# W_gate and W_up ahead of W_Q: another order of the first three loads and of their products in an attention and feed-forward decode kernel

## The chip, the cores and the metric

The kernel runs on one core of a Trainium2 chip. The metric is the device time of one execution in microseconds (us); the time before is a median of three runs.

## The reference

One token of each of 4 sequences goes through a layer norm, and the normed row `xn` feeds two branches that are added to the input:

```python
xn = _layernorm(x, axis=-1)                       # x: (4, 1, 512)
return x + _A_ref(xn, A_k_cache, A_v_cache, A_wq, A_wo) + _B_ref(xn, B_w_gate, B_w_up, B_w_down)
# A: q = xn @ wq; k, v = last W = 4096 rows of the caches, 8 heads, each shared by 4 query heads
#    softmax(q k^T / sqrt(128)) v, then @ wo        (32 query heads of 128)
# B: (silu(xn @ w_gate) * (xn @ w_up)) @ w_down     (F = 1792)
```

All tensors are bf16. The keys and values that are read are 8 heads x 4 sequences x 4096 rows x 128 numbers each, 32 MiB for the keys and as much for the values; the weights add some 14 MB.

## The kernel before, in words

The work goes in eight groups, one for each key/value head (`HKV = 8`, named 1 to 8 on the computing engines and 0 to 7 on the loading side, where K0 and V0 are the loads of the first group). A group's keys are 4 MiB in one of two buffers `kbuf`, its values 4 MiB in one of two buffers `vbuf`. The loads are all issued by SyncE (SP in the profile) in `on_sync`, in program order on one queue: W_Q (L256), W_gate (L257), W_up (L258), then `load(g)` for g = 0 to 7 (keys at L241, the last head's in two halves at L245 and L246, values at L251), then W_down (L261, L263) and W_O in five pieces (L254). Two buffers are used twice: W_Q lies in the second value buffer (`WQ` is a view of `VB1`), and W_O in the first key buffer.

SP waits in three places. Before the keys of head g >= 2 it waits until the transposes of head g - 2 are done (`s_tr`), before the values of head g >= 2 until that head's value products are done (`s_pv`), and before the values of head 1, which overwrite W_Q, until the query products are done (`s_q`, L248). The input row X is loaded by ScalarE (ACT) at L271.

VectorE (DVE) and ACT compute the layer norm (L306 to L312), TensorE (PE) transposes it (L377), DVE copies it to `XnT` (L314). Then come the three products with a weight that stands on its own semaphore each, in `on_tensor`: the queries (L381 to L386: wait for W_Q, 4 x 32 matmuls into `q_ps`, then `s_q`), and in one loop gate and up (L387 to L399: for each weight a wait and 21 x 4 matmuls into `gate_ps` and `up_ps`, then `s_gu`). A row of W_Q in a partition is 4 x 4096 bf16 numbers, 32 KB without a gap; one of W_gate or W_up is 4 x 1792 numbers, 14 KB.

DVE takes the queries out of PSUM in two copies after waiting for `s_q` (L315 to L319: `QT` for all heads and `QC` for the first group), then, after ACT's exponential of the gate (L290), forms the SwiGLU product `guT` in four steps (L355 to L362). PE waits for `guT` (L404) before its loop over the groups.

In a group PE transposes the keys in 16 chunks (L415) into PSUM, DVE and ACT share the copies of them to SBUF (L326 and L280), PE forms the scores (L427), a maximum is taken and subtracted, ACT takes the exponential (L283), and PE multiplies with the values (L448). Between the steps PE runs filler matmuls (`spin`, L470). After the groups come the down product (L474), a permutation of the heads (L528), the product with W_O (L474 and L478), two copies to `y`, and the store (L302).

## Time and profile before

| | |
|---|---|
| time, median of 3 runs | 195.13 us (195.11 to 195.15) |
| time of the profiled execution | 195.3 us |
| its span, first to last instruction | 193.9 us |
| bytes read from HBM | 81.01 MB, 418 GB/s over the span |
| busy share of the span | PE 84%, DVE 51%, ACT 36%, POOL 3% |
| mean granted clock of PE | 0.991 |

The page cuts the span into 40 slices of 4.85 us. Digits are busy shares in tenths. Beside them stands what the 16 DMA engines moved in each slice. The chain of work is followed backward from the last instruction and given in order of time: a start, a length, and what ran or was waited for. In a timeline a row is a start, a length, an engine, a line, an operation with the tile written and the tiles read, and in square brackets the idle time of the engine before it with what ended it. A row of a load names its queue (SPq) and the time that issuing took; its landing is found among the DMA issues, in us after the issue. Rows of a wait name who waited, for whom, the us in total, the times, and the longest. Rows of a stretch (windows) give the limits, the length, the busy time of the five engines, the granted clock, the DMA share and GB/s.

### The profile page before, as it was taken

The numbers are of one execution on the slowest core, as the hardware profiler recorded it, in microseconds if no ns is written. First come the engines' busy times: TensorE is split into PE (matmuls) and PEld (weight loads), VectorE is DVE, ScalarE is ACT, GpSimd is POOL, SyncE is SP. The second block draws the span as 40 slices with busy tenths as digits, with TensorE's granted clock in tenths as the row PEclk, the third lists the DMA queues.
The fourth block names the chain that finished last, engine by engine and source line by source line (L and its number), as shares of the span: only waits on it lengthen the run. The fifth ranks groups of instructions, "written<-read, shape, count | busy, mean of one in ns | idle before, by whom it ended". The sixth has DMA issues, their size and how long they took to land.

```text
span 193.9 us, 6951 instructions
## 1 busy us (share of the span) xinstructions
PE 163.8 (84%) x3179; PEld 135.2 (70%) x3179; DVE 99.0 (51%) x200; ACT 69.1 (36%) x100; POOL 5.7 (3%) x33
## 2 busy tenths in 40 slices
PE   0038973998699899999999799989996999999995
PEld 0038973997389759956994699469945994997532
DVE  0200011578258737870885188428842884588230
ACT  5510000243416343525461446234623462363421
POOL 7300000000000000000000000000000000000000
PEclk9999999999789999999999999999999999999999
DMA  6999999999999999999999999999999999999993
GB/s 216 433 438 429 427 429 433 429 433 429 433 429 436 426 429 436 426 433 433 439 433 433 433 433 433 433 433 433 433 433 433 433 426 433 439 433 433 436 400 131
DMA packets 3800, 81.14 MB, mean 418 GB/s; under 512 B 440, under 2 KB 576, under 8 KB 832
## 3 DMA queue, kind: packets, MB, share of 16 engines
q1 hardware_dynamic: 3776, 81.00, 97.5%
q8 instruction: 8, 0.13, 0.2%
q10 hardware_dynamic: 16, 0.01, 0.0%
HBM read 81.01 MB, written 0.00 MB: 418 GB/s over the span
## 4 chain that ended last, share of the span: by engine, by line
PE 48%; DMA 44%; DVE 5%; issue 1%; SPq 1%; ACT 0%; DVEq 0%
DMA kbuf<-in_A_k_cache_dram 44%; PE ps_kt L415 23%; PE ps_s L427 8%; PE ps_o L448 5%; PE ps_kt L470 4%; DVE kT L326 2%; PE ps_s L439 2%; PE ps_s L464 2%; DVE mx L332 2%; PE ps_s L478 1%; PE ps_s L474 1%; PE ps_s L461 1%; PE ps_kt L454 1%; PE ps_kt L434 0%; ACT s L298 0%
## 5 line engine op out<-in xcount | busy, mean ns | idle before, releaser
L415 PE MATMUL ps_kt<-ident,kbuf 128*128 128x128 bf16 x1024 | 78.2, 224 | 9.0 <-DMA kbuf<-in_A_k_cache_dram 8.5
L415 PEld LDWEIGHTS ps_kt<-ident,kbuf 128*128 128x128 bf16 x1024 | 60.6, 100 | 11.2 <-DMA kbuf<-in_A_k_cache_dram 9.6
L326 DVE COPY kT<-ps_kt 128x1024 bf16<-128x1024 bf16 x88 | 57.6, 686 | 18.5 <-PE ps_kt L415 16.5
L280 ACT ACTIVATE kT<-ps_kt 128x1024 bf16<-128x1024 bf16 x40 | 40.9, 1023 | 52.9 <-PE ps_kt L415 52.9
L427 PE MATMUL ps_s<-qC,kT 128*128 128x16 bf16 x1024 | 44.8, 170 | 2.6 <-DVE kT L326 1.9
L427 PEld LDWEIGHTS ps_s<-qC,kT 128*128 128x128 bf16 x1024 | 38.4, 97 | 4.6 <-DVE kT L326 4.1
L283 ACT ACTIVATE p<-ps_s 128x512 bf16<-128x512 f32 x32 | 16.5, 603 | 34.0 <-PE ps_s L439 34.0
L332 DVE TENSOR_REDUCE mx<-ps_s 128x16 f32<-128x512 f32 x32 | 22.0, 689 | 6.9 <-PE ps_s L427 5.0
L470 PE MATMUL ps_kt<-own,ones 128*128 128x512 bf16 x82 | 20.7, 380 | 0.0
L448 PE MATMUL ps_o<-vbuf,p 128*32 128x256 bf16 x512 | 19.1, 289 | 0.3
L448 PEld LDWEIGHTS ps_o<-vbuf,p 128*32 128x32 bf16 x512 | 14.9, 101 | 5.9 <-ACT p L283 4.2
L343 DVE TENSOR_REDUCE dsum<-ps_kt 128x16 f32<-128x256 f32 x8 | 3.4, 425 | 28.6 <-PE ps_kt L454 28.6
L454 PE MATMUL ps_kt<-p,ones 128*32 128x256 bf16 x64 | 16.9, 287 | 0.0
L470 PEld LDWEIGHTS ps_kt<-own,ones 128*128 128x128 bf16 x82 | 6.6, 97 | 7.0 <-issue 1.1
L377 PE MATMUL ps_s<-i,xn 4*128 4x4 f32 x4 | 0.6, 254 | 10.1 <-DVE xn L312 10.1
L439 PE MATMUL ps_s<-cm,own 128*128 128x512 bf16 x32 | 8.3, 380 | 1.0 <-DVE cm L340 1.0
L377 PEld LDWEIGHTS ps_s<-i,xn 4*128 4x128 f32 x4 | 0.6, 208 | 10.1 <-issue 10.1
L454 PEld LDWEIGHTS ps_kt<-p,ones 128*32 128x32 bf16 x64 | 6.6, 103 | 0.1
L290 ACT ACTIVATE ex<-ps_o 128x84 f32<-128x84 f32 x1 | 0.2, 240 | 17.5 <-PE ps_o L396 17.5
L439 PEld LDWEIGHTS ps_s<-cm,own 128*128 128x128 bf16 x32 | 2.5, 97 | 5.3 <-DVE cm L340 3.4
L286 ACT ACTIVATE osb<-ps_o 128x256 f32<-128x256 f32 x8 | 3.1, 383 | 8.2 <-PE ps_kt L454 8.2
L464 PE MATMUL ps_s<-sel,osb 128*128 128x16 f32 x36 | 5.8, 275 | 0.0
(83 smaller groups left out, 84.8 us busy)
## 6 DMA issues: line engine op xcount, KB each, us to landing
vbuf<-in_A_v_cache_dram SPq DMA_DIRECT2D x8, 4096.0 KB, 30.5
kbuf<-in_A_k_cache_dram SPq DMA_DIRECT2D x7, 4096.0 KB, 27.4
vbuf<-in_A_wq_dram SPq DMA_DIRECT2D x1, 4096.0 KB, 12.4
kbuf<-in_A_k_cache_dram SPq DMA_DIRECT2D x2, 2048.0 KB, 25.3
kbuf<-in_A_wo_dram SPq DMA_DIRECT2D x1, 2048.0 KB, 27.2
wg_sb<-in_B_w_gate_dram SPq DMA_DIRECT2D x1, 1792.0 KB, 16.1
wu_sb<-in_B_w_up_dram SPq DMA_DIRECT2D x1, 1792.0 KB, 20.9
wd_sb<-in_B_w_down_dram SPq DMA_DIRECT2D x1, 1664.0 KB
```

What stands on the lines that cost most here:

```text
L280: eng.activation(KT[:, c % 4], kt_ps[c % 3], ACT.Copy).then_inc(s_ev[c], 1)
L283: eng.activation(P[:, BT * q:BT * (q + 1), :], ps_S[q][:].rearrange("p (t n) -> p t n", n=NH), ACT.Exp, scale=SCALE).then_inc(s_p[q], 1)
L326: eng.tensor_copy(KT[:, c % 4], kt_ps[c % 3]).then_inc(s_ev[c], 1)
L332: eng.tensor_reduce(mx[:, q, :], ps_S[q][:].rearrange("p (t n) -> p n t", n=NH), AX.X, ALU.max)
L343: eng.tensor_reduce(dsum[:], den_ps.rearrange("p (t n) -> p n t", n=NH), AX.X, ALU.add).then_inc(s_dn, 1)
L415: last = eng.transpose(kt_ps[c % 3][:, k, :], KB[u][:, CH * c + k, :], ident[:])
L427: last = mm(ps_S[q][:, NH * t:NH * (t + 1)], KT[:, c % 4, k, :], QC[:], start=(t == 0), stop=False, skip_group_check=True)
L439: mm(ps_S[q][:].rearrange("p (t n) -> p t n", n=NH), own[:], CM[:].unsqueeze(1).to_broadcast([128, BT, NH]), start=False, stop=True, skip_ ...
L448: mm(O_ps[32 * n:32 * n + 32, :], P[:, t:t + 2, :].rearrange("p t n -> p (t n)"), VB[u][:, t:t + 2, :].rearrange("p t d -> p (t d)"), star ...
L454: last = mm(den_ps[32 * n:32 * n + 32, :], ones[:, 0:32], P[:, DT * e:DT * (e + 1), :].rearrange("p t n -> p (t n)"), start=(e < 4), stop= ...
L464: last = mm(O2_ps, Osb[:, Dh * h:Dh * (h + 1)], sel[:, NH * h:NH * (h + 1)], start=(h == 0), stop=(h == 1), skip_group_check=True)
L470: mm(ps_kt[k][:], ones[:], own[:].unsqueeze(1).to_broadcast([128, 4, 128]), skip_group_check=True)
```

## The change

Blocks change places on three engines; no instruction is added, removed or given another shape.

- On SP, W_Q is loaded third, behind W_gate and W_up.
- On PE, the block of the query products stands behind the loop of gate and up.
- On DVE, the wait for `s_q` and the two copies of the queries stand behind the SwiGLU chain, just ahead of the loop over the groups.

```diff
@@ on_sync
-        eng.dma_start(WQ, wq_ap).then_inc(d_wq, 16)
         eng.dma_start(WG[:], wg_ap).then_inc(d_wg, 16)
         eng.dma_start(WU[:], wu_ap).then_inc(d_wu, 16)
+        eng.dma_start(WQ, wq_ap).then_inc(d_wq, 16)
         for g in range(HKV):
             load(g)
@@ on_vector
         eng.tensor_copy(XnT[:], xT_ps.rearrange("p (c b) -> p c b", b=B)).then_inc(s_xnT, 1)
-        eng.wait_ge(s_q, 1)
-        eng.tensor_copy(QT[:, 0:HKV].rearrange("p k (b h) -> p k b h", b=B),
-                        q_ps.rearrange("p (k h b) -> p k b h", k=HKV, b=B))
-        eng.tensor_copy(QC[:].rearrange("p (b h) -> p b h", b=B),
-                        q_ps.rearrange("p (k h b) -> p k b h", k=HKV, b=B)[:, 0])
...
         eng.tensor_tensor(guT[:, :, 0:B], up_ps, gs[:], ALU.mult).then_inc(s_guT, 1)
+        eng.wait_ge(s_q, 1)
+        eng.tensor_copy(QT[:, 0:HKV].rearrange("p k (b h) -> p k b h", b=B),
+                        q_ps.rearrange("p (k h b) -> p k b h", k=HKV, b=B))
+        eng.tensor_copy(QC[:].rearrange("p (b h) -> p b h", b=B),
+                        q_ps.rearrange("p (k h b) -> p k b h", k=HKV, b=B)[:, 0])
         with eng.Fori(1, HKV + 1) as n:
@@ on_tensor
         eng.wait_ge(s_xnT, 1)
-        eng.wait_ge(d_wq, 16)
-        for c in range(NC):
-            for h in range(HQ):
-                last = mm(q_ps[:, h * B:(h + 1) * B], WQ[:, c, h * Dh:(h + 1) * Dh], XnT[:, c, :],
-                          start=(c == 0 and h == 0), stop=(c == NC - 1), skip_group_check=True)
-        last.then_inc(s_q, 1)
         for w, d, o in ((WG, d_wg, gate_ps), (WU, d_wu, up_ps)):
             eng.wait_ge(d, 16)
...
         last.then_inc(s_gu, 1)
+        eng.wait_ge(d_wq, 16)
+        for c in range(NC):
+            for h in range(HQ):
+                last = mm(q_ps[:, h * B:(h + 1) * B], WQ[:, c, h * Dh:(h + 1) * Dh], XnT[:, c, :],
+                          start=(c == 0 and h == 0), stop=(c == NC - 1), skip_group_check=True)
+        last.then_inc(s_q, 1)
         for q in range(NB):
             eng.sem_inc(s_p[q], 1)
```

## The prediction, made before the run

> **What bounds the kernel now.** I read the page from the top: busy shares, then the slices with the DMA rows, then the chain of work that ended last, and after these the waits.

> ```profile
> span 193.9 us, 6951 instructions
> PE 163.8 (84%) x3179; PEld 135.2 (70%) x3179; DVE 99.0 (51%) x200; ACT 69.1 (36%) x100; POOL 5.7 (3%) x33
> ...
> DMA  6999999999999999999999999999999999999993
> GB/s 216 433 438 429 427 429 433 429 433 429 433 429 436 426 429 436 426 433 433 439 433 433 433 433 433 433 433 433 433 433 433 433 426 433 439 433 433 436 400 131
> DMA packets 3800, 81.14 MB, mean 418 GB/s; under 512 B 440, under 2 KB 576, under 8 KB 832
> ```

> See the row of DMA digits: after the first slice (4.85 us wide) every slice but the last stands at 9, and the row below stays between 426 and 439 GB/s until the last two. The span is a stream of 81 MB with a start and a tail. PE at 84% is close behind, so I look at who waits for whom late in the span.

> ```profile
> 2.18 30.22 DMA kbuf<-in_A_k_cache_dram
> 32.45 2.74 PE ps_kt L415 x24
> ...
> 83.81 26.45 DMA kbuf<-in_A_k_cache_dram
> 110.30 1.51 PE ps_kt L415 x24
> ...
> 120.96 28.01 DMA kbuf<-in_A_k_cache_dram
> 149.01 1.51 PE ps_kt L415 x24
> ...
> 189.61 2.54 PE ps_s L478 x36
> 192.17 0.41 DVE y_sb L370
> ```

> ```profile
> PE ps_kt L415 <- DMA kbuf<-in_A_k_cache_dram: 4.0, 3, 1.8
> ```

> ```profile
> PEld ps_s L478 <- DMA kbuf<-in_A_wo_dram: 0.4, 2, 0.2
> ```

> The first of these fences is the chain in order of time. It passes through K loads whose "duration" is mostly a queue: the K load issued at 83.81 takes 26.45 us, though about 9.8 us (worked out below) is the transfer and the rest is what stood ahead of it. The second is the waits between 84 and 150 us: PE stands three times, 4.0 us in all, for K. The third is the tail: in the last matmuls PE waits twice, 0.4 us in all, for W_O, the last weight of the stream. So from the fifth group on PE follows the stream, and whatever PE loses earlier is made good as long as it is under those 4.0 us. **The end moves only if the stream moves.**

> **The change, part by part.** SP issues the same 30 loads; three of them trade places. On PE 128 matmuls go behind 168, on DVE a wait and two copies go behind the SwiGLU chain. The rows of the start:

> ```profile
> 0.81 0.39 SPq L256 DMA_DIRECT2D vbuf<-in_A_wq_dram  x1
> 1.26 0.41 SPq L257 DMA_DIRECT2D wg_sb<-in_B_w_gate_dram  x1
> 1.71 0.43 SPq L258 DMA_DIRECT2D wu_sb<-in_B_w_up_dram  x1
> 2.18 0.64 SPq L241 DMA_DIRECT2D kbuf<-in_A_k_cache_dram  x1
> ...
> 3.52 0.61 SPq L241 DMA_DIRECT2D kbuf<-in_A_k_cache_dram  x1
> ...
> 7.92 0.68 DVE L306 BATCH_NORM_STATS2 st_bn<-x_sb 4x6 f32<-4x512 bf16 x1 [7.92 <-DMA x_sb<-in_A_x_dram]
> ...
> 10.76 0.17 DVE L314 CAST xnT<-ps_s 128x16 bf16<-128x16 f32 x1 [0.79 <-PE ps_s L377]
> ...
> 13.31 3.55 PE L384 MATMUL ps_s<-xnT,vbuf 128*128 128x4 bf16 x128 [2.59 <-DMA vbuf<-in_A_wq_dram]
> 16.89 0.54 SPq L251 DMA_DIRECT2D vbuf<-in_A_v_cache_dram  x1
> 16.90 0.29 DVE L316 CAST qT<-ps_s 128x128 bf16<-128x128 f32 x1 [5.96 <-PE ps_s L384]
> 17.11 0.17 DVE L318 CAST qC<-ps_s 128x16 bf16<-128x16 f32 x1
> ...
> 17.43 5.19 PE L396 MATMUL ps_o<-xnT,wg_sb 128*128 128x4 bf16 x84 [0.57 <-DMA wg_sb<-in_B_w_gate_dram]
> ...
> 22.70 5.18 PE L396 MATMUL ps_o<-xnT,wu_sb 128*128 128x4 bf16 x84
> 27.92 0.24 ACT L290 ACTIVATE ex<-ps_o 128x84 f32<-128x84 f32 x1 [17.45 <-PE ps_o L396]
> ...
> 29.54 0.25 DVE L362 TENSOR_TENSOR guT<-ps_o,gs 128x84 bf16<-128x84 f32 x1
> 32.45 2.74 PE L415 MATMUL ps_kt<-ident,kbuf 128*128 128x128 bf16 x24 [4.57 <-DMA kbuf<-in_A_k_cache_dram]
> ```

> ```profile
> vbuf<-in_A_wq_dram SPq DMA_DIRECT2D x1, 4096.0 KB, 12.4
> ...
> wg_sb<-in_B_w_gate_dram SPq DMA_DIRECT2D x1, 1792.0 KB, 16.1
> wu_sb<-in_B_w_up_dram SPq DMA_DIRECT2D x1, 1792.0 KB, 20.9
> ```

> *SP.* The issues cost 0.39, 0.41 and 0.43 us, so in any order K's first load is issued at 2.18. Landings, issue plus time to landing: W_Q 0.81 + 12.4 = 13.2, W_gate 17.4, W_up 22.6, and K 2.18 + 30.22 = 32.4, so 9.8 us for 4096 KB. The three together are 7680 KB in either order, so the third, now W_Q, lands at 22.6 and K at 32.4 as before. W_gate, now first, is 2304 KB ahead of where W_Q ended; at K's 9.8 us per 4096 KB that is 5.5 us, so it lands near 7.7 and W_up near 12. Term for the stream behind them: 0.

> *PE.* Gate needs xnT (10.76 + 0.17) and W_gate (7.7): it starts near 11.0 if X lands as now, earlier if X comes earlier; I take 11.0. Gate 5.2 to 16.2, up 5.2 to 21.4 (W_up is there since 12). The queries wait for W_Q at 22.6, take 3.55 and end at 26.2. Now the three products end at 22.70 + 5.18 = 27.9. PE is free 1.7 us earlier and then waits for K till 32.4 all the same: 6.2 us of idling in place of 4.57. What is saved is idle time. Term: 0.

> *DVE and ACT.* With up done at 21.4, the exponential and the four DVE steps take what they take from 27.92 to 29.79, so guT is ready near 23.3. The moved wait for the queries then holds DVE till 26.2. Queued behind it are the two copies (0.29 and 0.17, done by 26.7) and the first copy of kT, which needs the transposes after 32.45. Cover: 32.4 - 26.7 = 5.7 us. On ACT only the exponential moves, forward; behind it is group 1, which starts after K. PE's own wait for guT is over before its queries end. Term: 0, and without the cover it would be PE's delay less the 4.0 us of waits above.

> *SP behind the queries.* V1 overwrites W_Q's buffer, so SP holds V1's issue until the queries are done: 16.89 becomes 26.2. Ahead of V1 in the stream stand K0, V0 and K1, the last of them issued at 3.52; K0 ends at 32.4, so by 9.8 us each K1 ends near 52. V1 still comes 25 us before the stream would run dry. K2, next on SP, waits for the first group's transposes far beyond 26. Term: 0.

> *The start of the stream.* This part the trace of before does not show: first rows of 14 KB instead of 32 KB.

> ```profile
> 1.50:13.20 11.70, 0.61 (x4) 0.55 (x4) 1.71 (x5) 6.06 (x8) 4.80 (x23) 1.00 0.97 397
> 13.20:17.40 4.20, 3.55 (x128) 3.50 (x128) 0.37 (x2) 0.00 (x0) 0.00 (x0) 1.00 1.02 437
> ```

> The last column is GB/s. W_Q's stretch runs at 397, W_gate's, with the short rows, at 437, so short rows are no slower once they flow. W_Q's deficit is 11.7 x 40 / 437 = 1.07 us: the wait for the first packet and the slow first ones. If that goes with the length of a first row (14336 / 32768 = 0.44), 0.6 us comes back; if it is a fixed latency, nothing; a loss as large, 0.6 us, is the other end, since nothing in these rows excludes that a later row or a later packet meets the slow start instead. Nearest row: the 437, where a change of row length cost nothing. I take 0.

> [...]

> **Sum.** 0 for the stream, PE, DVE and SP, 0 for the start: span 193.9, as now. The profiled execution took 195.3 us, 1.4 more than its span and 0.2 more than the median of 195.13; with the median as base the forecast is **195.1 us**.

> **The rivals.**

> *B, the short rows shorten the start.* The 1.07 us shrink with the first row. For it: the first slice's 216 GB/s. Against it: the deficit includes the wait for a first packet, which no row length changes. Price -0.6 at most, about -0.5: 194.6.

> *C, code loading strikes the slowest queue (slower).*

> ```profile
> q1 hardware_dynamic: 60, 0.86, 101.9%
> q8 instruction: 1, 0.02, 2.9%
> ```

> ```profile
> q8 instruction: 8, 0.13, 0.2%
> ```

> W_gate took 17.4 - 13.2 = 4.2 us, W_up, of the same size, 22.6 - 17.4 = 5.2. In W_up's stretch (first fence, 18.5 to 20.5 us) lies one of the eight packets of code that the second fence counts for the whole span. [...] PE's code is reordered; if a packet now falls on an engine that is already the last, all that follows lands 1.0 us later: 196.1. It decides once two fall on one engine that had at most one. Against it: as many instructions, so as many packets, at about the same count of instructions.

> [...]

> *D, PE comes late (slower).* PE's idling before K0 grows to 6.2 us. The 24 transposes after today's 4.57 us take 2.74 us against 1.51 at 110.30, so PE already starts group 1 slow; a further such loss, 1.2 us per 24, stays under the 4.0 us of waits. It decides only beyond these: 5 us lost give 196.1.

> [...]

> **How the numbers follow.** Chances: no change 0.58, B 0.22, C 0.16, D 0.04. A difference of 0.2%, 0.39 us, is about what a measurement of this kernel can tell from no change; the forecast's own spread is 194.8 to 195.5. Faster 0.22 (B), within 0.2% 0.58, slower 0.20 (C and D). The range takes in the forecast and B, 0.80: 194.4 to 195.6, its upper end a little under the 0.6 us loss at the start; C and D are left out.

> **What would show it.** Right: W_gate lands near 7.7, W_Q near 22.6, K0 still ends PE's wait at about 32.4, V1 is issued near 26 with no dip in the GB/s row, and PE still waits for K at about 110 and 149. B is right if W_gate lands at 7.2 and K0 near 31.9, with everything behind as much earlier. C shows as K landings late by 1 us from one point on, D as PE's waits for K before 149 gone. I am wrong altogether if the GB/s row dips after the start or the tail behind W_O changes length.

## The result, and the profile after

The change made the kernel slower: 195.87 us (median of 7 runs, 195.63 to 195.99) against 195.13 (7 runs, 195.04 to 195.29); ratio 1.0036, 95% interval 1.0026 to 1.0046. The forecast was 195.1 with 194.4 to 195.6, so the time lies above the range.

The profiled execution took 195.99 us with a span of 194.6. First the page of after: the span, the DMA rows of the slices, the count of code packets.

```profile
span 194.6 us, 6951 instructions
...
DMA  6999999999999999999999999999999989999992
GB/s 194 434 437 428 431 434 431 438 428 448 445 428 434 421 424 441 424 431 445 438 438 431 431 431 438 438 431 431 438 431 431 431 381 431 482 431 385 438 404 94
...
q8 instruction: 8, 0.13, 0.2%
```

The stream is as dense as before from the second slice on, and as many code packets run beside it; only the first slice is a little lower (194 against 216 GB/s). The 381 and 385 GB/s near the end are no dips of after: over the same stretches, 155.7 to 160.5 and 175.1 to 180 us, both kernels move 386 and 383 GB/s. The landings of the first three loads, from the page's DMA issues (KB, then us from issue to landing):

```profile
vbuf<-in_A_wq_dram SPq DMA_DIRECT2D x1, 4096.0 KB, 21.7
...
wg_sb<-in_B_w_gate_dram SPq DMA_DIRECT2D x1, 1792.0 KB, 7.7
wu_sb<-in_B_w_up_dram SPq DMA_DIRECT2D x1, 1792.0 KB, 11.5
```

W_gate is issued at 0.81 and lands at 8.5, where 7.7 was forecast; W_Q, issued at 1.71, lands at 23.4 instead of 22.6. The timeline of after shows that all the rest of the start went as worked out:

```profile
7.17 0.68 DVE L306 BATCH_NORM_STATS2 st_bn<-x_sb 4x6 f32<-4x512 bf16 x1 [7.17 <-DMA x_sb<-in_A_x_dram]
...
10.23 5.18 PE L390 MATMUL ps_o<-xnT,wg_sb 128*128 128x4 bf16 x84 [0.27 <-DVE xnT L314]
...
15.27 5.17 PE L390 MATMUL ps_o<-xnT,wu_sb 128*128 128x4 bf16 x84
...
23.48 3.57 PE L397 MATMUL ps_s<-xnT,vbuf 128*128 128x4 bf16 x128 [3.03 <-DMA vbuf<-in_A_wq_dram]
27.08 0.54 SPq L251 DMA_DIRECT2D vbuf<-in_A_v_cache_dram  x1
...
33.16 2.74 PE L415 MATMUL ps_kt<-ident,kbuf 128*128 128x128 bf16 x24 [6.10 <-DMA kbuf<-in_A_k_cache_dram]
```

X comes 0.75 us earlier, gate and up are done at 20.4, the queries at 27.05, V1 is issued at 27.08, and PE idles 6.1 us before K0. But K0 lets PE start at 33.16 instead of 32.45: 0.71 us, about as much as the kernel lost, are there before the first group begins. PE makes them good: its third group begins with these rows, the first in before, the second in after.

```profile
73.21 1.45 PE ps_kt L415 x24
```

```profile
73.16 1.45 PE ps_kt L415 x24
```

The landings don't. When PE waits for the stream again, for its fifth keys, it is 0.71 us late once more (111.01 against 110.30), and so it stays to the end. From the chain of work of after, in order of time:

```profile
111.01 1.51 PE ps_kt L415 x24
...
149.66 1.51 PE ps_kt L415 x24
...
190.26 2.58 PE ps_s L478 x36
192.86 0.41 DVE y_sb L370
```

149.66 against 149.01 is 0.65 later, 192.86 against 192.17 is 0.69. The waits between 84 and 150 us are as before (4.4 us in three waits against 4.0), so PE follows the stream as it did:

```profile
PE ps_kt L415 <- DMA kbuf<-in_A_k_cache_dram: 4.4, 3, 1.8
```

Yet the stream did not move fewer bytes in the start. The same stretch as in the prediction, 1.5 to 13.2 us, in the windows of after:

```profile
1.50:13.20 11.70, 3.57 (x54) 3.52 (x55) 1.71 (x5) 6.06 (x8) 4.80 (x23) 1.00 1.00 395
```

395 GB/s against 397 are 0.02 MB, or 0.06 us. On the whole the 16 DMA engines are as far as before; what differs, as I read the views, is how far they are apart. In the DMA view of a short stretch 16 packets "under 512 B" stand at the end of each of these loads, whose rows are 14 KB and more. I read them as one for each engine, so that they count the engines that finish the load there. First before, W_Q's 16 ends from 12.0 us on; then after, W_gate's from 6.5 us on (one of the 11 is X's); then the run with W_up first (below), where two of the 16 are X's:

```profile
DMA packets 27, 0.19 MB, mean 373 GB/s; under 512 B 14, under 2 KB 14, under 8 KB 14
...
DMA packets 18, 0.23 MB, mean 459 GB/s; under 512 B 2, under 2 KB 2, under 8 KB 2
```

```profile
DMA packets 30, 0.27 MB, mean 389 GB/s; under 512 B 11, under 2 KB 11, under 8 KB 11
...
DMA packets 23, 0.29 MB, mean 410 GB/s; under 512 B 3, under 2 KB 3, under 8 KB 3
...
DMA packets 24, 0.30 MB, mean 430 GB/s; under 512 B 3, under 2 KB 3, under 8 KB 3
```

```profile
DMA packets 38, 0.32 MB, mean 451 GB/s; under 512 B 16, under 2 KB 16, under 8 KB 16
...
DMA packets 18, 0.24 MB, mean 348 GB/s; under 512 B 1, under 2 KB 1, under 8 KB 1
...
DMA packets 24, 0.33 MB, mean 471 GB/s; under 512 B 1, under 2 KB 1, under 8 KB 1
```

So read, in before 14 engines finish the first load within half a microsecond and two in the next. In after 10 finish by 7.2 us, three by 7.9 and three by 8.6: **three engines leave the start far behind.** With W_up first 14 finish by 7.2 us, one by 7.9 and one by 8.6: one engine is far behind.

The landing follows the last of the 16. In before that one falls between 12.8 and 12.9 us, W_Q lands at 13.2, and PE's wait for it ends at 13.31; in after it falls between 8.1 and 8.2 us, and W_gate lands at 8.5. Both landings come 0.3 to 0.4 us behind it, though the 16 spread over less than a microsecond in before (12.0 to 12.9) and over up to 1.7 us in after (6.5 to 8.2). That a landing is that of the last engine is my reading; the views name no engine.

### The profile page after: what moved, and what is told of

Read it like the earlier page. It is cut to its first block, busy times and chain, and to the rows that moved or that the text cites. A ratio compares the mean times of both kernels' runs of the same rounds, so it can differ in the third digit from the quotient of the medians.

```text
span 194.6 us, 6951 instructions
## 1 busy us (share of the span) xinstructions
PE 163.7 (84%) x3179; PEld 135.0 (69%) x3179; DVE 98.9 (51%) x200; ACT 69.1 (36%) x100; POOL 5.7 (3%) x33
## 2 busy tenths in 40 slices
DMA packets 3800, 81.14 MB, mean 417 GB/s; under 512 B 440, under 2 KB 576, under 8 KB 832
## 4 chain that ended last, share of the span: by engine, by line
PE 48%; DMA 44%; DVE 5%; SPq 1%; issue 1%; ACT 0%; DVEq 0%
DMA kbuf<-in_A_k_cache_dram 44%; PE ps_kt L415 23%; PE ps_s L427 8%; PE ps_o L448 5%; PE ps_kt L470 4%; DVE kT L321 2%; PE ps_s L439 2%; PE ps_s L464 2%; DVE mx L327 2%; PE ps_s L478 1%; PE ps_s L474 1%; PE ps_s L461 1%; PE ps_kt L454 1%; PE ps_kt L434 0%; ACT s L298 0%
## 5 line engine op out<-in xcount | busy, mean ns | idle before, releaser
L415 PE MATMUL ps_kt<-ident,kbuf 128*128 128x128 bf16 x1024 | 78.1, 223 | 10.6 <-DMA kbuf<-in_A_k_cache_dram 10.5
L415 PEld LDWEIGHTS ps_kt<-ident,kbuf 128*128 128x128 bf16 x1024 | 60.4, 99 | 13.0 <-DMA kbuf<-in_A_k_cache_dram 12.2
L377 PE MATMUL ps_s<-i,xn 4*128 4x4 f32 x4 | 0.6, 254 | 9.4 <-DVE xn L312 9.4
L377 PEld LDWEIGHTS ps_s<-i,xn 4*128 4x128 f32 x4 | 0.6, 206 | 9.3 <-issue 9.3
L397 PE MATMUL ps_s<-xnT,vbuf 128*128 128x4 bf16 x128 | 3.6, 166 | 3.0 <-DMA vbuf<-in_A_wq_dram 3.0
## 6 DMA issues: line engine op xcount, KB each, us to landing
vbuf<-in_A_v_cache_dram SPq DMA_DIRECT2D x8, 4096.0 KB, 30.7
kbuf<-in_A_k_cache_dram SPq DMA_DIRECT2D x7, 4096.0 KB, 27.9
vbuf<-in_A_wq_dram SPq DMA_DIRECT2D x1, 4096.0 KB, 21.7
wg_sb<-in_B_w_gate_dram SPq DMA_DIRECT2D x1, 1792.0 KB, 7.7
wu_sb<-in_B_w_up_dram SPq DMA_DIRECT2D x1, 1792.0 KB, 11.5
```

The source lines that it names most:

```text
L397: last = mm(q_ps[:, h * B:(h + 1) * B], WQ[:, c, h * Dh:(h + 1) * Dh], XnT[:, c, :], start=(c == 0 and h == 0), stop=(c == NC - 1), skip_g ...
L415: last = eng.transpose(kt_ps[c % 3][:, k, :], KB[u][:, CH * c + k, :], ident[:])
```

## The experiments

All times are medians of several rounds beside runs of before on the same chip, which took 195.12 to 195.18 us. Three theories stand in the expectations. S, held at the outset: the first load's start spreads the engines and the slowest of them sets every landing. C: the reordered products move code packets. P: the later query products hold something up. SxC, the later joint theory, joins S and C: a late engine sets the end only where it takes a code packet too.

### Which part of the change it is

**Order of the products alone.**

```diff
+        eng.dma_start(WQ, wq_ap).then_inc(d_wq, 16)
         eng.dma_start(WG[:], wg_ap).then_inc(d_wg, 16)
         eng.dma_start(WU[:], wu_ap).then_inc(d_wu, 16)
-        eng.dma_start(WQ, wq_ap).then_inc(d_wq, 16)
```

> Queue as before (W_Q, W_gate, W_up), products as after (gate, up, then queries). Theory S, the start: with 14 KB rows first the DMA engines leave the start further apart, and the slowest of them sets every landing; the order of the products costs nothing. S expects no difference from before, 195.1 us, K0 landing at 32.4 and W_Q at 13.2. Theory C, code packets: the reordered instructions of PE bring a code packet onto an engine that is late already; C expects the full 0.7 us here too, 195.9, with K0 at 32.4 and a later K landing 0.7 us late. Theory P, the later query products: V1 issued late or PE late; P expects 195.9 as well, with PE's waits for K before 149 us shorter than 4.0.

195.17 us, ratio 0.9996 (0.9987 to 1.0005); PE starts K0 at 32.34. The order of the products costs nothing, and C and P in the form given fall with it.

**Only one load with 14 KB rows ahead of W_Q.**

```diff
-        eng.dma_start(WU[:], wu_ap).then_inc(d_wu, 16)
         eng.dma_start(WQ, wq_ap).then_inc(d_wq, 16)
+        eng.dma_start(WU[:], wu_ap).then_inc(d_wu, 16)
```

> After with W_Q and W_up exchanged in the queue: only the first load has 14 KB rows. S, if the first load alone decides: as slow as after, 195.9, K0 at 33.1. If each short-row load adds its share: halfway, 195.5. C expects 195.9 too, so this run is for the size, not for the choice between them; a time of 195.1 would speak against S in the form 'the first row decides'.

195.83 us, ratio 1.0035 (1.0023 to 1.0047): the full loss. One expectation was missed: PE starts K0 at 32.56, and nearly all of the loss shows only behind it (the K of 110.30 in before comes at 111.04). So the first load decides, but its lateness needn't be seen at once.

**W_Q in two loads with 16 KB rows.**

```diff
-        eng.dma_start(WQ, wq_ap).then_inc(d_wq, 16)
+        eng.dma_start(WQ[:, 0:2, :], wq_ap[:, 0:2, :]).then_inc(d_wq, 16)
+        eng.dma_start(WQ[:, 2:4, :], wq_ap[:, 2:4, :]).then_inc(d_wq2, 16)
```

> Before, with W_Q as two loads of 2048 KB whose rows are 16 KB; the order of loads and products is that of before, and one more load is issued (0.4 us of SP, behind the first). S in the form 'the length of the first rows decides': slower by about what after is, 195.6 to 195.9, K0 at about 33. C and P: no difference from before, 195.1, K0 at 32.4. A rival within S, that it is where W_gate lies or its row of 14336 bytes, not a power of two: 195.1 too.

195.19 us, ratio 0.9999 (0.9990 to 1.0008). Rows half as long cost nothing, so S in the form "the length of the first rows decides" falls.

**Later loads held back till about 4 us.**

```diff
         eng.dma_start(WG[:], wg_ap).then_inc(d_wg, 16)
+        eng.wait_ge(s_dl, 1)
         eng.dma_start(WU[:], wu_ap).then_inc(d_wu, 16)
@@ on_gpsimd
         rows(0)
-        eng.drain()
+        eng.drain().then_inc(s_dl, 1)
```

> After, but SP issues W_up, W_Q and the rest only when GpSimd is through its first selects (about 4 us); W_gate's 8 rows on each engine last till about 7 us, so no engine runs out. S with the issue as its cause (an engine's first rows wait while the issue of the next loads and of X prepares theirs, and short rows run out sooner): the spread at W_gate's landing shrinks, W_gate lands near 7.7 instead of 8.5, and the time falls towards 195.2. S with the memory's first accesses as its cause: no change, 195.9. C: no change, 195.9.

195.91 us, ratio 1.0041 (1.0029 to 1.0053). What SP issues behind W_gate has no part in it. ACT's load of X, issued at 1.75 us in after, was not held back.

### What it is about the first load

**W_up first.** The two lines of W_gate and W_up on SP change places.

> After with W_gate and W_up exchanged in the queue (W_up, W_gate, W_Q). If the rows' layout is the cause (14336 bytes long, one right behind the other in memory), W_up does what W_gate did: 195.9 us, first load landing near 8.5, K0 near 33.1. If it is where W_gate in particular lies in memory, W_up may do without: 195.2, first load landing near 7.7.

195.19 us, ratio 1.0003 (0.9995 to 1.0012). The rows are as long and lie as close as W_gate's, but the loss is gone, though the last of the first load's 16 ends falls between 7.9 and 8.6 us, as in after. The rows' layout isn't the cause, and the end of the first load alone doesn't tell the time.

**W_Q first with rows of 14336 bytes.**

```diff
+        eng.dma_start(WQF[:, 0:7168], wq_f[:, 0:7168]).then_inc(d_wq, 16)
+        eng.dma_start(WQF[:, 7168:16384], wq_f[:, 7168:16384]).then_inc(d_wq2, 16)
```

> Before, with W_Q in two loads: first the leading 14336 bytes of every row, then the other 18432. Rows are as long as W_gate's, but start 32768 bytes apart. If the length of 14336 is the cause: 195.9, this load landing near 8.5. If it is how the rows lie (close behind one another, 14336 bytes apart): 195.1, landing near 7.7.

195.29 us, ratio 1.0011 (1.0002 to 1.0019): by the medians 0.17 us, about a quarter of the loss; the interval reaches up to half of it. The length of 14336 bytes is not the cause of the whole.

**W_gate first in two loads, rows of 8192 and 6144 bytes.**

```diff
-        eng.dma_start(WG[:], wg_ap).then_inc(d_wg, 16)
+        eng.dma_start(WGF[:, 0:4096], wg_f[:, 0:4096]).then_inc(d_wg, 16)
+        eng.dma_start(WGF[:, 4096:7168], wg_f[:, 4096:7168]).then_inc(d_wg2, 16)
```

> After, with W_gate in two loads: first the leading 8192 bytes of every row, then the other 6144. Rows start 14336 bytes apart as in after, but the first load's rows are a power of two long. If the length of 14336 is the cause: 195.2. If it is how the rows lie: 195.9, and engines still leave the start far apart.

195.38 us, ratio 1.0014 (1.0006 to 1.0023). Between the two expectations: some 0.26 us of the loss stay, so cutting W_gate in two goes with a smaller loss, and no rule of the length comes out.

**A quarter of W_Q ahead of W_gate.**

```diff
+        eng.dma_start(WQF[:, 0:4096], wq_f[:, 0:4096]).then_inc(d_wq, 16)
         eng.dma_start(WG[:], wg_ap).then_inc(d_wg, 16)
         eng.dma_start(WU[:], wu_ap).then_inc(d_wu, 16)
+        eng.dma_start(WQF[:, 4096:16384], wq_f[:, 4096:16384]).then_inc(d_wq2, 16)
```

> After, with a quarter of W_Q ahead: the leading 8192 bytes of every row of W_Q, then W_gate, W_up, and the rest of W_Q. If only the first load out of an idle stream matters and W_Q's rows lie well, this gives before's time with after's order of products: 195.2, K0 near 32.4. If W_gate's rows cost what they cost wherever they stand: 195.9. If short first rows as such cost (8 KB are shorter than after's 14): 195.9 or more.

195.00 us, ratio 0.9995 (0.9986 to 1.0003). As the second load W_gate costs nothing, here (195.00) as in before; whole and first it cost 0.7 us in the runs above (195.83 to 195.91). This is after's order of products with the loss undone; its interval against before includes 1, so it isn't a proved gain. The four runs from W_up first to this one were made on one chip, on which W_gate whole and first was not timed. The exchange of the declarations below has the loss and its absence on one chip.

**Tiles of W_gate and W_up exchanged in SBUF.**

```diff
-    WG = sb("wg_sb", [128, NC, F], BF16, 512)
     WU = sb("wu_sb", [128, NC, F], BF16, 512)
+    WG = sb("wg_sb", [128, NC, F], BF16, 512)
```

> After with the tiles of W_gate and W_up exchanged in SBUF: W_gate is loaded first, into the place where W_up was. W_up as the first load cost nothing. If the cause lies on the writing side (the place in SBUF): 195.2 us, K0 near 32.4. If it lies on the reading side (where W_gate lies in memory): 195.9, K0 near 33.1.

195.84 us, ratio 1.0035 (1.0022 to 1.0048): the place in SBUF isn't the cause. This run and the first of the next two share a chip.

**The two inputs declared in the other order**, once with W_gate first, once with W_up first.

```diff
-    for name in _INS:
+    for name in ('A_x', 'A_k_cache', 'A_v_cache', 'A_wq', 'A_wo', 'B_x', 'B_w_up', 'B_w_gate', 'B_w_down'):
...
+    args[6], args[7] = args[7], args[6]
```

> After with the two inputs W_gate and W_up declared in the other order, so that they may lie in memory in each other's place; nothing else is changed. If the place in memory is the cause and the order of declaration sets it: 195.2, K0 near 32.4. If the place in memory doesn't follow the order of declaration, or if it isn't the cause: 195.9, which leaves the two undecided.

> Queue W_up, W_gate, W_Q, and the two inputs declared in the other order, so that W_up lies where W_gate did in after. If the place in memory makes the slow start: 195.9 us, three engines over 1.1 us behind the first at the first load's landing, K0 near 33.1. If it is W_gate as such, or the other declaration cures it by itself: 195.2, K0 near 32.4.

W_gate first: 195.25 us, ratio 1.0005 (0.9996 to 1.0014). W_up first: 195.80, ratio 1.0032 (1.0021 to 1.0044). PE's first wait for K in the one and in the other:

```profile
32.50 2.74 PE L415 MATMUL ps_kt<-ident,kbuf 128*128 128x128 bf16 x24 [6.12 <-DMA kbuf<-in_A_k_cache_dram]
```

```profile
32.90 2.31 PE L415 MATMUL ps_kt<-ident,kbuf 128*128 128x128 bf16 x20 [5.93 <-DMA kbuf<-in_A_k_cache_dram]
```

The loss changes sides with the declaration: whichever weight is declared first of the two is the slow one to begin with. The late ends change sides too. Of the 16 ends of the first load, 14, 1 and 1 fall into the three stretches from 6.5 to 8.6 us with W_gate first, and 10, 3 and 3 with W_up first. In before, where W_Q goes first, all 16 fall between 12.0 and 13.0 us.

With the place in SBUF excluded, the likely reading is that the declaration changes **where the weight lies in memory**. That is inferred: no run gives an address, and what about such a place is slow isn't shown. How late K0 itself is differs among the runs that lost: 32.56 (W_Q second), 32.84 (tiles exchanged), 32.90 here, 33.16 in after.

### From the start to the end

**Less code.** Of the products of queries, gate and up only the first contraction step is kept, in after and in before:

```diff
-        for c in range(NC):
+        for c in range(1):
             for h in range(HQ):
...
-                for c in range(NC):
+                for c in range(1):
```

> After with only the first of the four contraction steps in the products of queries, gate and up (three quarters of these products are left out): PE has 444 instructions less, nearly two code packets of 16 KB. Theory S alone (the slowest start sets everything): 195.9 as after. Theory S with C (a late engine sets the end only when it also takes a code packet, and in after the last two of eight packets fall on late engines): fewer than eight instruction packets, the late landings of K behind 70 us gone or halved, 195.2 to 195.6, and the difference to the run of before with less code under 0.5 us.

> Before with the same three quarters of the products of queries, gate and up left out: the base for the run of after with less code. The stream is the same, PE is early and waits longer. Both theories: 195.1, or up to 0.3 less where a code packet less falls on the slowest engine.

After: 195.89 us (195.20 to 196.47), ratio 1.0037 (1.0024 to 1.0049). Before: 195.15, ratio 1.0000 (0.9992 to 1.0009). The difference is 0.74, not under 0.5 as the joint theory said. But that nearly two code packets would go was the author's estimate, and how many went isn't shown, so the times alone settle nothing. The start does tell something. PE's first transposes, of after and then of before:

```profile
32.00 2.74 PE L415 MATMUL ps_kt<-ident,kbuf 128*128 128x128 bf16 x24 [8.71 <-DMA kbuf<-in_A_k_cache_dram]
```

```profile
31.26 2.74 PE L415 MATMUL ps_kt<-ident,kbuf 128*128 128x128 bf16 x24 [8.24 <-DMA kbuf<-in_A_k_cache_dram]
```

K0 is 0.74 us late with less code too, and 0.74 us are still there in the time (195.89 against 195.15).

**Hardly any code.** Before, after, and W_up first with a short program on PE, which leaves out most of the arithmetic (parts of the edit):

```diff
-            for k in range(CH):
+            for k in range(1):
                 last = eng.transpose(kt_ps[c % 3][:, k, :], KB[u][:, CH * c + k, :], ident[:])
...
-            for t in range(0, NT, 2):
+            for t in range(0, 8, 2):
...
-            for _ in range(n):
+            for _ in range(1):
```

> Before with a short program on PE: one of four contraction steps in the first products, one transpose, one score matmul and a sixteenth of the value product in place of eight and all, one filler in place of five (so most of the arithmetic is left out; the loads and their order are those of before). Fewer than three code packets instead of eight. If the code packets set the slowest engine's end (theory SxC), the last landing of W_O comes up to 1.3 us earlier: 193.8 us; if they don't, 195.1.

> After with the same short program. Both theories expect it slower than the short before: S by 0.7 us, SxC by what its slowest engine is late at W_gate's landing more than the short before's at W_Q's, about 0.9.

> The queue W_up, W_gate, W_Q with the same short program. With all its code this order took before's time, though one engine left the start 1.5 us behind the first. SxC (that engine takes no code packet, so the eight that do hide it): without code packets nothing hides it, slower than the short before by 0.8 to 0.9 us. A late single engine made good in another way: no difference to the short before.

196.24 us (ratio 1.0050, 1.0037 to 1.0063), 195.96 (1.0051, 1.0032 to 1.0071), 196.11 (1.0057, 1.0037 to 1.0077). Two expectations of the times were missed: no run is faster than before, and by the medians the short before is the slowest of the three, not the fastest. The times say nothing on the question, because PE is slow in the tail; the fillers that are gone may be the reason, which isn't shown. In the first of these runs the 16 matmuls with W_O take 1.90 us, where before has 1.05 us for the same work:

```profile
186.53 1.90 PE L473 MATMUL ps_s<-kbuf,oP 128*32 128x512 bf16 x16 [0.34 <-DMA kbuf<-in_A_wo_dram]
```

The landings of K do answer. PE now waits for each of them, so its first transposes date them. In the three runs, in the order above:

```profile
31.31 0.50 PE L415 MATMUL ps_kt<-ident,kbuf 128*128 128x128 bf16 x3 [8.30 <-DMA kbuf<-in_A_k_cache_dram]
51.80 0.50 PE L415 MATMUL ps_kt<-ident,kbuf 128*128 128x128 bf16 x3 [4.64 <-DMA kbuf<-in_A_k_cache_dram]
71.13 0.50 PE L415 MATMUL ps_kt<-ident,kbuf 128*128 128x128 bf16 x3 [3.50 <-DMA kbuf<-in_A_k_cache_dram]
```

```profile
32.05 0.50 PE L415 MATMUL ps_kt<-ident,kbuf 128*128 128x128 bf16 x3 [8.71 <-DMA kbuf<-in_A_k_cache_dram]
51.94 0.50 PE L415 MATMUL ps_kt<-ident,kbuf 128*128 128x128 bf16 x3 [4.04 <-DMA kbuf<-in_A_k_cache_dram]
71.26 0.50 PE L415 MATMUL ps_kt<-ident,kbuf 128*128 128x128 bf16 x3 [3.49 <-DMA kbuf<-in_A_k_cache_dram]
```

```profile
32.29 0.50 PE L415 MATMUL ps_kt<-ident,kbuf 128*128 128x128 bf16 x3 [8.72 <-DMA kbuf<-in_A_k_cache_dram]
52.03 0.50 PE L415 MATMUL ps_kt<-ident,kbuf 128*128 128x128 bf16 x3 [3.89 <-DMA kbuf<-in_A_k_cache_dram]
71.35 0.50 PE L415 MATMUL ps_kt<-ident,kbuf 128*128 128x128 bf16 x3 [3.50 <-DMA kbuf<-in_A_k_cache_dram]
```

Each of the three has a single code packet between 40 and 46 us. From 2 to 40 us the DMA views of the first and the third show none, and the second has the third's program on PE:

```profile
q8 instruction: 1, 0.02, 1.0%
```

W_up, whose stretch in before had the code packet that the prediction priced at 1.0 us, lands 19.8 us after its issue in the first of these runs instead of 20.9, so that packet went with a landing 1.1 us later:

```profile
wu_sb<-in_B_w_up_dram SPq DMA_DIRECT2D x1, 1792.0 KB, 19.8
```

With all its code the first row of each kernel is at 32.45, 33.16 and, W_up first, 32.53:

```profile
32.53 2.74 PE L415 MATMUL ps_kt<-ident,kbuf 128*128 128x128 bf16 x24 [5.91 <-DMA kbuf<-in_A_k_cache_dram]
```

That is 1.14, 1.11 and 0.24 us later than with the short program. In each of the three, two code packets fall between 2 and 32 us:

```profile
q8 instruction: 2, 0.03, 0.4%
```

The reading is that with W_up first most of their delay is hidden behind the one late engine (0.24 us are left), and that in after it is added in full (1.11 us), because a packet strikes an engine that is behind already, which is likelier with three such engines than with one. It is an inference: the views don't name the engine of a packet.

## Why the prediction was wrong

- *What bounds the kernel*: right. The stream's landings moved by 0.65 to 0.71 us and the end by 0.69; PE's waits before 150 us stayed (4.4 us).
- *PE, DVE, SP behind the queries, each at 0*: right. The order of the products alone gave 0.9996.
- *The stream behind the three loads, at 0*: right for the bytes (395 against 397 GB/s to 13.2 us) and wrong for the landings. "The three together are 7680 KB in either order, so the third, now W_Q, lands at 22.6 and K at 32.4" takes the stream for one pipe. As read here, it is 16 engines, and a landing is that of the last: with the same 7680 KB ahead of K0, W_Q landed at 23.4 and K0 at about 33.1.
- *The start, "I take 0"*: this is the step that failed. Its own bounds were -0.6 and +0.6 for want of a row; the term measured +0.7 (0.71 at K0, 0.74 in the time), beyond even the upper bound, and the range, which ended at 195.6, didn't hold that bound either. The nearest row, the 437 GB/s, is a mean rate of a stream in flow and could not show it, since the loss, as read here, is a spread between engines: three of the 16 ends of the first load come between 7.9 and 8.6 us, 10 by 7.2. The row that bore on it was the one that C used: a landing 1.0 us late while the stream flowed on. Why three engines start late stays open.
- *B (faster through short rows)*: refuted. Rows of 16, 14 and 8 KB of W_Q first gave 0.9999, 1.0011 and 0.9995. The wait for the first packet was the same with rows of 32 KB and of 14 KB: it came at 1.8 us in before and in after.
- *C (a code packet on an engine that is already last)*: its direction came out, its size roughly (1.0 us against 0.74), and its cause didn't. It said that reordered code would bring the packet there; reordered code alone cost nothing (0.9996). That a packet counts only on the engine that is last is the author's supposition, and no run names the engine of a packet; the runs showed W_up landing 1.1 us earlier with the short program, without a packet (19.8 against 20.9). As read above, the first load made engines late that packets strike anyway; so that C came near the time is mostly luck.
- *D*: right to be small; PE idled 6.1 us and its first 24 transposes took 2.74 us, as before.

The prediction held a fixed latency at the start possible. The first packets agree with that: before and after both show them from about 1.8 us on, 0.6 us after SP was done with issuing the first load (0.81 + 0.39). But the start is more than its first packets: with the same row lengths it costs 0 or 0.7 us, by which of two weights goes first and which is declared first.

## What to carry to other kernels

Here, with a stream on 16 DMA engines as the bound, equal bytes didn't mean equal landings: 395 against 397 GB/s to 13.2 us, and K0 0.71 us late. So look at how far the ends of a load are apart (the counts of its last small packets), not only at the GB/s. As read here, a delay counts in full only if it falls on an engine that is already among the last; a late start cost nothing with W_up first (195.19) and 0.74 us in after. Which load goes first is worth a trial on the chip for each candidate, and a reason in terms of its row length is worth little here.

## What the runs showed of the hardware that was not expected

- Which of two weights of the same size and shape is loaded first costs 0 or 0.7 us, and the order in which the inputs are declared decides which of them it is (195.87 with W_gate first and 195.25 after the exchange; 195.19 and 195.80 with W_up first).
- In after the lateness of the start isn't made good in the full stream: 0.71 us at K0 are 0.69 us at the last copy. With the short program 0.74 us at K0 are 0.14 us at K1, behind one code packet.
- A code packet (16 KB: 0.13 MB in 8) went with a landing of W_up 1.1 us later (20.9 against 19.8 us after its issue) and with a step to K1 1.16 us longer (20.49 against 19.33 in the short before). Two ahead of K0 went with no more: K0 is at 32.45 us in before, behind two, and at 31.31 with the short program, behind none, 1.14 us apart.
